# A two-layer decode block with its backward pass: the weight gradients begin inside the last attention's backward

## The chip, the core and the metric

One core of a Trainium2 chip runs the whole kernel. The metric is the device time of one execution in microseconds (us); eight executions of the kernel before have a median of 446.25 us (442.68 to 447.71). The engines are TensorE (PE; its weight loads are shown apart, as PEld), VectorE (DVE), ScalarE (ACT), GpSimd (Pool) and SyncE (SP), which here only issues DMAs. Each runs its own instructions in order and waits on semaphores for the others. SP issues DMAs on one queue, Pool on another; both feed the same 16 DMA engines.

## The reference

Four layers act on one token x of 1024 numbers, in the order A, B, A, B, with the same weights each time:

```python
x = x + A(layernorm(x))   # q = x@wq, 32 heads over 4 kv heads, softmax over the last 4096 keys, @wo
x = x + B(layernorm(x))   # h = x@w1 + b1; h*tanh(softplus(h)) @ w2
x = x + A(layernorm(x))
x = x + B(layernorm(x))
```

The output is x and, for a given gradient of it, the gradients of x, of the k and v caches (4 x 32768 x 128 each), of wq (1024 x 4096), wo (4096 x 1024), w1 (1024 x 3584), b1 and w2 (3584 x 1024), all in bf16. Outside of the last 4096 positions a cache's gradient is zero, so 28672 of 32768 rows in `out_2` and `out_3` are plain zeros that have to be written.

## The kernel before, in words

The layers are named A1, B2, A3, B4 on the way forward; the backward pass goes B4, A3, B2, A1. Weights pass through a ring of six 512 KB buffers (`ring`) or stay on the chip (`wq_b`, most of `wo_b`, K, V). The schedule is written out by hand: the program's order is each engine's order, and only waits are added.

Zero stores are single jobs of 512 KB (112 in all, `zero_jobs`). They are spread as filler for the DMA engines. `bg_zeros` (L180) puts them on Pool's queue behind a small copy that waits for a stage's value; `zeros` (L167) and `zeros2` (L171, two jobs per DMA, from `area["zero"]` inside `wo_b`) put them on SP's queue. The table `Z` says how many go where.

The last attention's backward is `attn_bwd` with `first=False`. It computes do = g @ wo^T (steps `T`, transpose a stored block, and `M`, multiply), then dP from V (`rows_mm`), ds, its transpose (`half_T`), dq from K (`qrow`, `yq`, `qacc`, `dq_bf`), dn from wq (`nrow`, `yr`, `rows_sel2`) and g0 through `ln_bwd`. Between its steps `warm` issues matmuls whose results nobody reads.

Each weight gradient is an outer product of two layers' row vectors, two rows deep. The vectors lie as columns, so they are first spread (copies on Pool into a zeroed `spread` tile), transposed on TensorE and copied out of PSUM: that is `spread_rows` (L1038), called through `tall_left`, `tall_right` and `rows_put`. Five such preparations for dW2 and dW1 are popped by `nextprep` between the last `M` steps and behind `rows_mm`.

Behind `attn_bwd` the PSUM pools are released, one pool `pair` of four 4 KB tiles is made, and the jobs run: 14 half chunks of dW2, 16 of dW1 (woven with 8 of dV behind the first 8), 16 of dWo, 16 of dWq woven with 8 of dK. A chunk is four matmuls into two `pair` tiles and two copies into a staging slot; `evac` gives each copy to VectorE or ScalarE by running totals. Every second chunk of a weight gradient issues its store on SP (1 MB, or 896 KB for dW1). Staging slots are used in turn from the list `slots`: two in `wo_b`, two in the ring, two in V, then eight in `wq_b`. dWq has a home instead, the parts of `wq_b` in their order. dK is stored in four 1 MB DMAs behind its last chunk. The preparations for the later gradients and five zero jobs are inserted between the jobs by position.

Of the kernel before, what the change touches and what calls it, by code (L numbers as in the profile page):

```python
# [14 lines left out]
P = 128  # L15
# [8 lines left out]
def kernel(  # L24
# [142 lines left out]
    def zeros(n):  # L167
        for _ in range(min(n, len(zero_jobs))):
            nc.sync.dma_start(zero_job(1), zt[:])

    def zeros2(n):  # L171

        while n > 0 and zero_jobs:
            k = 2 if zero_jobs[0][1] % 2 == 0 else 1
            nc.sync.dma_start(zero_job(k), area["zero"][:, 0:k * ZC])
            n -= k
# [92 lines left out]
        mm(acc.col(k), lhsT, vec.to_broadcast([P, R16]), start, stop)  # L269

    def acc_tile(n):
        return pacc.tile([P, n], FP32, name="acc", tag="acc")

    def sm_tile(m, n):
        return pacc.tile([m, n], FP32, name="sm", tag="sm")

    def mm(out_ap, lhsT, rhs, start, stop, **kw):
# [75 lines left out]
    def ln_bwd(dn_ps, n32, rstd, g_col, name, nxt):  # L353

        tt = work.tile([P, 2 * TD], FP32, name="tt")
        nc.vector.tensor_copy(tt[:, 0:TD], dn_ps)
        nc.vector.tensor_mul(tt[:, TD:], tt[:, 0:TD], n32[:])
        sps = sm_tile(P, 2 * TD)
        nc.tensor.matmul(sps[:], lhsT=onesD, rhs=tt[:], start=True, stop=True)
        if nxt == "A1":  # L360
            warm(5)
        if nxt == "B2":
            hook("ln")
        ab = work.tile([P, 2], FP32, name="ab")
        nc.vector.reduce_sum(ab[:], sps[:].rearrange("p (a b) -> p a b", a=2), axis=AX.X)
        t2 = work.tile([P, TD], FP32, name="t2")
        nc.vector.scalar_tensor_tensor(out=t2[:], in0=n32[:], scalar=ab[:, 1:2], in1=tt[:, 0:TD],
                                       op0=ALU.mult, op1=ALU.subtract, reverse1=True)
        gx = work.tile([P, TD], FP32, name="gx")
        nc.vector.tensor_scalar(out=gx[:], in0=t2[:], scalar1=ab[:, 0:1], scalar2=rstd[:, 0:1], op0=ALU.subtract, op1=ALU.mult)  # L370
        g_new = keep.tile([P, TD], FP32, name=f"g_{name}")
        nc.vector.tensor_add(g_new[:], g_col[:], gx[:])
        g_bf = pair_col("g" + nxt[0], nxt, TD)
        nc.vector.tensor_copy(g_bf, g_new[:])
        return g_new, g_bf
# [278 lines left out]
    def hook(nm):  # L654
        if nm in hooks:
            hooks.pop(nm)()
# [205 lines left out]
    def attn_bwd(g_col, g_bf, lname, sv, first, nxt):  # L862
# [30 lines left out]
        def M(i):  # L893
            c = late[i]
            w = held.pop(c)
            for dch in range(TD):
                mv(dacc, 2 * c + 1, w[:, 1, dch * P:(dch + 1) * P], g_bf[:, dch:dch + 1], False, dch == TD - 1)
            if i == 1:
                for j in range(4):
                    mm(dacc.cols(j, 16)[:, 0:13:4], de[:, j * P:(j + 1) * P], ident_bf[:, 0:P:32], False, True)  # L900
            if first and i in (1, 3, 5):
                fill(1, ["V", "K", "wq"], "a")
            if not first and i:
                nextprep()

        T(0)
        for c in range(8, NR):
# [8 lines left out]
        if not first:  # L916
            after_do()
            prep.extend([
                lambda: tall_left("w2", "a", 0),
                lambda: tall_left("w2", "a", 1),  # L920
                lambda: tall_right("w2", "gB"),
                lambda: rows_put(area["R1"], 0, "nB", "rep"),
                lambda: rows_put(area["R1"], 1, "dh", "pieces"),
            ])

        for i in range(2, len(late) + 1):
            if i < len(late):
# [2 lines left out]
        if first:  # L930
            pre.extend(w2_load(c) for c in range(NB - 1))
            bg_zeros(Z["A3d"], g_bf)
            fill(100, ["V"])
        else:
            after_stream()
            zeros(Z["A1d"][0])
            zeros2(Z["A1d"][1])

        do_p = work.tile([P, 2, NO], BF16, name="do_p")
        dcols = dacc.cols(0, HQ).rearrange("p (c t) -> p t c", t=2)  # L940
# [26 lines left out]
        if first:  # L967
            fill(3, ["K", "wq"], "a")
        else:
            after_v()  # L970
            nc.sync.dma_start(area["p3"], out_5[0:P, :])
            nextprep(100)
            warm(3)
        scr = kp()
        sdp = work.tile([P, 2], FP32, name="sdp")
        lps = sm_tile(P, 1)
# [7 lines left out]
        nc.vector.tensor_copy(sd[:], lps[:])  # L984
        ds = sv["p"] if first else area["ds"]
        dsT = kp().rearrange("p (j x) -> p j x", x=P)
        qrow = acc_tile(512)
        for hf in range(2):
            hs = slice(hf * 512, (hf + 1) * 512)
            nc.vector.scalar_tensor_tensor(out=ds[:, hs], in0=hv[hf][:], scalar=sd[:, 0:1], in1=sv["p"][:, hs], op0=ALU.subtract, op1=ALU.mult)  # L990
# [1 line left out]
        if first:  # L992
            fill(100, ["K"], "av")
        else:
            warm(4)
        for hf in range(2):
            half_T(ds, dsT, hf, "va"[hf])
        for j in range(TJ):
            for c in range(NC):
                mm(qrow[32 * c:32 * c + 32, :], dsT[:, j, 32 * c:32 * c + 32], kv["K"][:, :, 4 * j + c, :],  # L1000
                   j == 0, j == TJ - 1, tile_position=(0, 32 * c))
        yq = rows_copy(qrow, "v")
        if first:
            fill(2, ["wq"], "a")
        else:
            warm(3)
        qacc = sm_tile(P, HQ)
        for g in range(G):
            mm(qacc[:, 8 * g:8 * g + 8], yq[:, g * P:(g + 1) * P], fold[:, 8 * g:8 * g + 8], g == 0, True)
# [1 line left out]
        nc.scalar.activation(dq_bf, qacc[:], ACT.Copy, scale=scale)  # L1011
        if first:
            fill(100, ["wq"], "av")
        nrow = acc_tile(512)
        for h in range(HQ):
            for half in range(2):
                row_mm(nrow, 2 * half + h % 2, dq_bf[:, h:h + 1],
                       wq_b[:, 4 * half:4 * half + 4, h // 16, (h % 16) * P:(h % 16 + 1) * P], h < 2, h >= HQ - 2)
        nps = sm_tile(P, TD)
        yr = rows_copy(nrow, "v")  # L1020
        if first:
            hook("copy")
        rows_sel2(yr, Cols8(nps, True))
# [11 lines left out]
        nc.gpsimd.dma_start(out_flat.rearrange("(n p) -> n p", p=P), rt[0:n, :])  # L1035


    def spread_rows(n, put, dst, pairwise=False):  # L1038

        sp = area["spread"][pools["sturn"] % 2]  # L1040
        pools["sturn"] += 1
        for l in range(2):
            put(sp.rearrange("p j (q x) -> p j q x", q=4), l)
        ps = psum1([P, 8, P], BF16, "rw")
        for j in range(n):
            nc.tensor.transpose(ps[:, j, :], sp[:, j, :], ident_bf[:])  # L1046
        o, i = dst, ps[:, 0:n, :].rearrange("p j x -> p (j x)")
        if pairwise:
            o, i = dst.rearrange("p (c x t) -> p c t x", x=P, t=2), ps[:, 0:n, :].rearrange("p (c t) x -> p c t x", t=2)
        evac(o, i, 0.69, 1.0, None if "pair" in pools else "a")  # L1050

    def rows_put(R, side, kind, how):

# [141 lines left out]
    def after_do():  # L1195
# [1 line left out]
        area["spread"] = [s.rearrange("p (j x) -> p j x", x=P) for s in (s0, s1)]  # L1197
        area["R1"] = r1.rearrange("p (s x) -> p s x", s=2)
        pools["sturn"] = 0
        nc.gpsimd.memset(wo_flat[:, 0:2048], 0.0)  # L1200
        area["zero"], *more = cut_up(wo_flat, 8192, (4096,) * ((NR - 4) // 2))
        nc.gpsimd.memset(area["zero"], 0.0)
        slots.extend(more)
        dw_tall("w2", TF, out_8.rearrange("(c p t) d -> c p t d", p=P, t=4))
        dw_wide(lambda: area["R1"], 256, F // 2, out_6)
# [8 lines left out]
        slots.extend(cut_up(vf, 8192, (4096,) * 2))  # L1214

    prep = []
    def nextprep(n=1):
        for _ in range(min(n, len(prep))):
            prep.pop(0)()

    Z = dict(B2a=1, B2={0: 1, 4: 1, NW2 - 2: 4}, A3=14, B4=[3, 3, 2, 2, 2, 2, 5], A3c=6, A3d=28, B4w={1: 1, 4: 1, 13: 3}, W1=0, W1m=(8, 13), A1c=3, A1d=(7, 16))


    x1 = None
# [76 lines left out]
            nc.vector.tensor_copy(db_row[:, :, t], dbps[:])  # L1301
        nc.gpsimd.dma_start(out_7.rearrange("(c x) -> c x", x=2 * P), db_row.rearrange("c p t -> c (p t)"))

    g0, g0b = attn_bwd(g1, g1b, "A1", sA1, False, "X0")
    level()
    col_out(g0b, TD, out_1[0, 0, :])
    top(None)
    pacc.release()
    pt.release()
    pools["pair"] = ctx.enter_context(tc.tile_pool(name="pair", bufs=4, space=bass.MemoryType.PSUM))  # L1310

    def r3(nm):
        return area[nm].rearrange("p (g d) -> p g d", g=G)

    slots.extend(wq_b[:, t, :, :].rearrange("p h j -> p (h j)") for t in range(TD))
    stage = {}

    def take(nm):
        stage[nm] = jobs[:]
        del jobs[:]  # L1320

    take("w")
    dkv(area["p3"], r3("do3"), sA1["p"], r3("do1"), out_3, True)
    take("v")
    dw_tall("wo", HQ, out_5.rearrange("(c p t) d -> c p t d", p=P, t=4))
    take("o")
    dkv(sA3["ds"], r3("q3"), sA1["ds"], r3("q1"), out_2, False)
    take("k")
    dw_wide(lambda: area["Rq"], 512, 2048, out_4, wq_t)
    take("q")  # L1330
    late_prep = [
        lambda: row_layout(sA3["dorep"], "do3"),
        lambda: row_layout(sA1["dorep"], "do1"),
        lambda: tall_left("wo", "o", 0),
        lambda: tall_left("wo", "o", 1),
        lambda: tall_right("wo", "gA"),
        lambda: row_layout(sA3["qrep"], "q3"),
        lambda: row_layout(sA1["qrep"], "q1"),
        lambda: rows_put(area["Rq"], 0, "nA", "rep"),
        lambda: rows_put(area["Rq"], 1, "dq", "heads"),  # L1340
        db1_out,
        x4_out,
    ]

    def weave(a, b, n):
        while a or b:
            jobs.extend(a[0:n])
            jobs.extend(b[0:1])
            del a[0:n], b[0:1]

    jobs.extend(stage["w"][:NW2 + 8])
    weave(stage["w"][NW2 + 8:], stage["v"], 1)
    jobs.extend(stage["o"])
    weave(stage["q"], stage["k"], 2)
    for at, f in zip((8, 11, 24, 27, 30, 40, 43, 46, 49, 51, 53), late_prep):
        jobs.insert(at, f)
    for at, n in ((24, 2), (27, 2), (33, 1)):
        jobs.insert(at, lambda n=n: zeros2(n))
    run(1000)
    zeros2(1000)  # L1360
    assert not zero_jobs
# [30 lines left out]
```

## Time and profile before

| | |
|---|---|
| median of 8 runs | 446.25 us (442.68 to 447.71) |
| the profiled execution | 446.17 us, of which the span of the core is 444.4 |
| PE / DVE / ACT / Pool busy | 321.7 / 235.3 / 214.5 / 66.3 us |
| HBM read, written | 70.27 MB, 99.10 MB |
| mean granted TensorE clock | 0.733 of full |

The profile is of one execution. Times in it count from the span's start. A line such as L278 is the line of a helper, so groups are told apart by their tiles: `ops` is a weight gradient's PSUM tile, `rw` a row preparation's, `tps` a weight transpose, `wps` a `warm` matmul. A row "out<-in" names the tiles; what stands in brackets is the engine's idle time just before, and who ended it. The DMA share is the mean busy share of the 16 DMA engines in a stretch.

### The profile page before, as it was taken

How to read it: one execution, taken by the hardware profiler on the slowest of the kernel's cores; microseconds unless marked ns; L12 is line 12 of the kernel's file. 1: busy time of each engine (PE TensorE's matmuls, PEld its weight loads, DVE VectorE, ACT ScalarE, POOL GpSimd, SP SyncE). 2: the span in 40 equal slices, each digit the busy share in tenths (PEclk: the TensorE clock that was granted, in tenths of full speed). 3: DMA queues.
4: the chain of work that ended last, by engine and by line, in shares of the span. 5: the costliest groups of instructions: out<-in, count | busy, mean ns of one | idle time of the engine just before them, and what ended most of it. 6: DMA issues, size and time to landing. Idle time of an engine off the chain costs nothing. (4 is left out here: it accounts for less than half of the span.)

```text
span 444.4 us, 11638 instructions
## 1 busy us (share of the span) xinstructions
PE 321.7 (72%) x5020; PEld 219.1 (49%) x5020; DVE 235.3 (53%) x487; ACT 214.5 (48%) x253; POOL 66.3 (15%) x164
## 2 busy tenths in 40 slices
PE   1555855497887979988997587795967698585850
PEld 0332524497375979975876586764431132211110
DVE  3134201187251756674547373461439989897860
ACT  1122100065142867876855242523218877796860
POOL 2000000012420312252332010117010010000000
PEclk9997555566697998998998558986985555555555
DMA  8999999999999899999999999999979999999778
GB/s 317 420 421 415 407 405 372 407 371 392 397 405 344 328 348 370 386 411 412 416 408 383 416 330 380 308 411 421 424 305 374 418 413 409 402 412 396 299 307 354
DMA packets 44336, 170.13 MB, mean 383 GB/s; under 512 B 4448, under 2 KB 11644, under 8 KB 37500
## 3 DMA queue, kind: packets, MB, share of 16 engines
q1 hardware_dynamic: 31888, 124.79, 71.0%
q0 software_dynamic: 12352, 44.58, 25.6%
q8 instruction: 39, 0.64, 0.5%
q14 instruction: 13, 0.11, 0.1%
q10 hardware_dynamic: 44, 0.01, 0.0%
HBM read 70.27 MB, written 99.10 MB: 381 GB/s over the span
## 5 line engine op out<-in xcount | busy, mean ns | idle before, releaser
L278 PEld LDWEIGHTS <-ring 128*128 128x128 bf16 (+2 forms) x1828 | 59.5, 101 | 33.9 <-DMA ring<-in_B_w_dram 12.8
L195 ACT COPY ring<-tps 128x1024 bf16<-128x1024 bf16 (+1 forms) x40 | 37.6, 962 | 29.4 <-PE tps L242 29.2
L185 POOL DMA_DIRECT2D out_dram<-zt x84 | 44.4, 532 | 39.8 <-DMA out_dram<-zt 34.3
L242 PE MATMUL tps<-ident_bf,ring 128*128 128x128 bf16 x528 | 40.0, 232 | 6.3 <-DMA ring<-in_B_w_dram 5.1
L685 ACT COPY ring<-tps 128x1024 bf16<-128x1024 bf16 x28 | 28.3, 1012 | 30.9 <-PE tps L675 23.1
L698 DVE CUSTOM_DVE_ANT_0 ring<-ring,gbc 128x1024 bf16<-128x1024 bf16 x28 | 33.7, 1220 | 15.2 <-PE acc L278 14.2
L192 DVE CAST wq_b<-ops 128x1024 bf16<-128x1024 f32 (+1 forms) x36 | 39.2, 1127 | 4.5 <-DMA out_dram<-wq_b 2.8
L195 ACT CAST wq_b<-ops 128x1024 bf16<-128x1024 f32 (+1 forms) x40 | 38.3, 1015 | 5.8 <-DMA out_dram<-wq_b 2.8
L242 PEld LDWEIGHTS <-ring 128*128 128x128 bf16 x528 | 33.7, 105 | 8.2 <-DMA ring<-in_B_w_dram 5.4
L278 PE MATMUL ops<-V 2*128 2x512 bf16 (+1 forms) x160 | 32.2, 603 | 5.7 <-DVE K L192 1.5
L192 DVE COPY ring<-tps 128x1024 bf16<-128x1024 bf16 (+1 forms) x30 | 19.6, 663 | 29.3 <-PE tps L242 28.9
L278 PEld LDWEIGHTS <-V 128*128 128x128 bf16 (+2 forms) x448 | 17.0, 102 | 33.1 <-issue 31.2
L195 ACT COPY K<-tps 128x1024 bf16<-128x1024 bf16 x17 | 16.6, 1024 | 28.9 <-PE tps L242 28.9
L278 PE MATMUL ops<-wo_b 2*128 2x512 bf16 x120 | 24.7, 570 | 8.1 <-ACT wq_b L195 3.0
L675 PE MATMUL tps<-ident_bf,ring 128*128 128x128 bf16 x224 | 24.8, 280 | 0.7 <-DMA ring<-in_B_w_dram 0.7
L278 PE MATMUL acc<-a_pair,ring 128*128 128x16 bf16 x448 | 16.0, 173 | 10.7 <-DMA ring<-in_B_w_dram 9.6
L192 DVE COPY K<-tps 128x1024 bf16<-128x1024 bf16 x15 | 10.2, 688 | 24.2 <-PE tps L242 24.2
L278 PE MATMUL q<-wq_b,nA_pair 128*32 128x512 bf16 x128 | 10.1, 439 | 17.0 <-DMA wq_b<-in_A_wq_dram 17.0
L278 PEld LDWEIGHTS <-wo_b 2*128 2x128 bf16 (+1 forms) x232 | 9.0, 99 | 26.0 <-issue 23.8
L195 ACT CAST K<-ops 128x1024 bf16<-128x1024 f32 x17 | 17.1, 1012 | 7.7 <-PE ops L278 7.5
L192 DVE CAST K<-ops 128x1024 bf16<-128x1024 f32 x15 | 18.3, 1222 | 3.3 <-PE ops L278 3.2
L294 DVE COPY ring<-acc 128x512 f32<-128x512 f32 x6 | 4.1, 691 | 28.8 <-PE acc L278 28.8
(319 smaller groups left out, 564.8 us busy)
## 6 DMA issues: line engine op xcount, KB each, us to landing
out_dram<-zt POOLq DMA_DIRECT2D x84, 512.0 KB, 10.2
ring<-in_B_w_dram SPq DMA_DIRECT2D x42, 512.0 KB, 7.6
ring<-in_B_w_dram SPq DMA_DIRECT2D x32, 448.0 KB, 6.6
out_dram<-wo_b SPq DMA_DIRECT2D x13, 1024.0 KB, 8.5
out_dram<-wq_b SPq DMA_DIRECT2D x12, 1024.0 KB, 4.9
ring<-in_A_wo_dram SPq DMA_DIRECT2D x20, 512.0 KB, 7.9
wq_b<-in_A_wq_dram SPq DMA_DIRECT2D x8, 1024.0 KB, 21.2
out_dram<-wq_b SPq DMA_DIRECT2D x7, 896.0 KB, 5.2
```

The source lines that it names most:

```text
L185: nc.gpsimd.dma_start(zero_job(1), zt[:])
L192: nc.vector.tensor_copy(out_ap, in_ap)
L195: nc.scalar.copy(out_ap, in_ap)
L242: nc.tensor.transpose(ps[:, b, :], ap, ident_bf[:])
L278: nc.tensor.matmul(out_ap, lhsT=lhsT, rhs=rhs, start=start, stop=stop, skip_group_check=True, **kw)
L294: nc.vector.tensor_copy(yr, bank[:])
L675: nc.tensor.transpose(self.ps[c][:, b, :], w[:, 1, b * P:(b + 1) * P], ident_bf[:])
L685: nc.scalar.copy(self.w[c][:, 1, :], self.ps.pop(c)[:].rearrange("p b c -> p (b c)"))
L698: nc.vector.tensor_tensor_reduce(out=w[:, 0, :], in0=w[:, 0, :], in1=gbc[:], scale=1.0, scalar=0.0, op0=ALU.mult, op1=ALU.add, accum_out=s ...
```

## The change

`spread_rows` is cut in two: Pool's copies are put at once (`put_rows`), and the transposes and the copy out of PSUM come when `finish_rows` is called. Two puts stand ahead of the last `T`/`M` steps of the last attention, and the finishes stand behind `rows_mm`. The memset of the zero area moves from `after_do` to behind ds.

The code that made the pool `pair` and the job list becomes `tail`, which is called inside `attn_bwd` when ds is issued. From there on `acc_tile` and `sm_tile` take their tiles from `pair`, and eight calls of `run(1)` stand between the remaining steps and behind them, in place of `warm`. `wq_b` joins the slots behind `nrow` (hook `wq`), so behind the sixth chunk.

The zero jobs are dealt out anew: one less in B2's pass over w2, two less in B4, one more each in the W2 and W1 passes of the backward, 18 single jobs instead of 23 behind the loads of the last attention, and 11 instead of 5 between the weight gradients. The preparations get new positions in the job list.

```diff
     def acc_tile(n):
+        if "pair" in pools:
+            return psum1([P, n], FP32, "acc")
         return pacc.tile([P, n], FP32, name="acc", tag="acc")
...
@@ ln_bwd
         if nxt == "B2":
             hook("ln")
+        if nxt == "X0":
+            run(1)
...
@@ attn_bwd
-            if not first and i:
-                nextprep()
...
+            put_rows()
+            put_rows()
...
             after_stream()
-            zeros(Z["A1d"][0])
-            zeros2(Z["A1d"][1])
+            zeros(Z["A1d"])
...
             nc.sync.dma_start(area["p3"], out_5[0:P, :])
-            nextprep(100)
-            warm(3)
+            finish_rows()
+            put_rows()
+            finish_rows()
+            put_rows()
...
-        qrow = acc_tile(512)
+        qrow = acc_tile(512) if first else None
...
-            warm(4)
+            finish_rows()
+            put_rows()
+            nc.gpsimd.memset(area["zero"], 0.0)
+            hook("tail")
+            run(1)
         for hf in range(2):
             half_T(ds, dsT, hf, "va"[hf])
+        if not first:
+            finish_rows()
+            run(1)
+            qrow = acc_tile(512)
...
-            warm(3)
+            finish_rows()
+            run(1)
         qacc = sm_tile(P, HQ)
...
+        if not first:
+            run(1)
         nrow = acc_tile(512)
         for h in range(HQ):
+            if not first and h == HQ // 2:
+                run(1)
...
+        yr = rows_copy(nrow, "v")
+        if not first:
+            hook("wq")
+            run(1)
         nps = sm_tile(P, TD)
-        yr = rows_copy(nrow, "v")
...
@@ spread_rows
         for l in range(2):
             put(sp.rearrange("p j (q x) -> p j q x", q=4), l)
-        ps = psum1([P, 8, P], BF16, "rw")
...
+        def finish():
+            ps = psum1([P, 8, P], BF16, "rw")
+            for j in range(n):
+                nc.tensor.transpose(ps[:, j, :], sp[:, j, :], ident_bf[:])
...
+        ready.append(finish)
...
@@ after_do
-        nc.gpsimd.memset(wo_flat[:, 0:2048], 0.0)
+        for s in (s0, s1):
+            nc.gpsimd.memset(s, 0.0)
         area["zero"], *more = cut_up(wo_flat, 8192, (4096,) * ((NR - 4) // 2))
-        nc.gpsimd.memset(area["zero"], 0.0)
...
-    Z = dict(B2a=1, B2={0: 1, 4: 1, NW2 - 2: 4}, A3=14, B4=[3, 3, 2, 2, 2, 2, 5], A3c=6, A3d=28, B4w={1: 1, 4: 1, 13: 3}, W1=0, W1m=(8, 13), A1c=3, A1d=(7, 16))
+    Z = dict(B2a=1, B2={0: 1, 4: 1, NW2 - 2: 3}, A3=14, B4=[2, 2, 2, 2, 2, 2, 5], A3c=6, A3d=28, B4w={1: 1, 4: 1, 7: 1, 10: 1, 12: 2}, W1=0, W1m=(2, 8, 13), A1c=3, A1d=18)
...
+    def tail():
+        top(None)
+        pacc.release()
+        pt.release()
+        pools["pair"] = ctx.enter_context(tc.tile_pool(name="pair", bufs=4, space=bass.MemoryType.PSUM))
+        level()
...
+        base = stage["w"][:NW2 + 8] + weave(stage["w"][NW2 + 8:], stage["v"], 1) + stage["o"] + weave(stage["q"], stage["k"], 2)
+        side = {
+            8: [lambda: row_layout(sA3["dorep"], "do3")],
...
+            16: [lambda: zeros2(2)],
...
+            40: [lambda: zeros2(2)],
...
+    hooks.update(tail=tail, wq=lambda: slots.extend(wq_b[:, t, :, :].rearrange("p h j -> p (h j)") for t in range(TD)))
+    g0, g0b = attn_bwd(g1, g1b, "A1", sA1, False, "X0")
+    run(1)
+    col_out(g0b, TD, out_1[0, 0, :])
     run(1000)
```

More of the change, by code (lines that the diff above doesn't have):

```diff
@@ L271, in acc_tile @@
     def acc_tile(n):
+        if "pair" in pools:
+            return psum1([P, n], FP32, "acc")
         return pacc.tile([P, n], FP32, name="acc", tag="acc")
     def sm_tile(m, n):
+        if "pair" in pools:
+            return psum1([m, n], FP32, "sm")
         return pacc.tile([m, n], FP32, name="sm", tag="sm")
@@ L1035, in col_out, with finish_rows @@
         nc.gpsimd.dma_start(out_flat.rearrange("(n p) -> n p", p=P), rt[0:n, :])
+    ready = []
+    def finish_rows():
+        ready.pop(0)()
     def spread_rows(n, put, dst, pairwise=False):
@@ L1043, in spread_rows @@
             put(sp.rearrange("p j (q x) -> p j q x", q=4), l)
-        ps = psum1([P, 8, P], BF16, "rw")
[L1045 to L1050, printed above, removed]
+        def finish():
+            ps = psum1([P, 8, P], BF16, "rw")
+            for j in range(n):
+                nc.tensor.transpose(ps[:, j, :], sp[:, j, :], ident_bf[:])
+            o, i = dst, ps[:, 0:n, :].rearrange("p j x -> p (j x)")
+            if pairwise:
+                o, i = dst.rearrange("p (c x t) -> p c t x", x=P, t=2), ps[:, 0:n, :].rearrange("p (c t) x -> p c t x", t=2)
+            evac(o, i, 0.69, 1.0, None if "pair" in pools else "a")
+        ready.append(finish)
     def rows_put(R, side, kind, how):
@@ L1216, with put_rows @@
     prep = []
-    def nextprep(n=1):
-        for _ in range(min(n, len(prep))):
-            prep.pop(0)()
-    Z = dict(B2a=1, B2={0: 1, 4: 1, NW2 - 2: 4}, A3=14, B4=[3, 3, 2, 2, 2, 2, 5], A3c=6, A3d=28, B4w={1: 1, 4: 1, 13: 3}, W1=0, W1m=(8, 13), A1c=3, A1d=(7, 16))
+    def put_rows():
+        prep.pop(0)()
+    Z = dict(B2a=1, B2={0: 1, 4: 1, NW2 - 2: 3}, A3=14, B4=[2, 2, 2, 2, 2, 2, 5], A3c=6, A3d=28, B4w={1: 1, 4: 1, 7: 1, 10: 1, 12: 2}, W1=0, W1m=(2, 8, 13), A1c=3, A1d=18)
     x1 = None
@@ L1302, in db1_out @@
         nc.gpsimd.dma_start(out_7.rearrange("(c x) -> c x", x=2 * P), db_row.rearrange("c p t -> c (p t)"))
[L1304 to L1310, printed above, removed]
     def r3(nm):
         return area[nm].rearrange("p (g d) -> p g d", g=G)
-    slots.extend(wq_b[:, t, :, :].rearrange("p h j -> p (h j)") for t in range(TD))
     stage = {}
@@ L1320, in take @@
         del jobs[:]
[L1322 to L1343, printed above, removed]
@@ L1345, in weave @@
     def weave(a, b, n):
+        out = []
         while a or b:
-            jobs.extend(a[0:n])
-            jobs.extend(b[0:1])
+            out.extend(a[0:n])
+            out.extend(b[0:1])
             del a[0:n], b[0:1]
[L1351 to L1358, printed above, removed]
+        return out
@@ new lines, in tail @@
+    def tail():
[4 more added lines that the diff above has]
+        level()
+        take("w")
+        dkv(area["p3"], r3("do3"), sA1["p"], r3("do1"), out_3, True)
+        take("v")
+        dw_tall("wo", HQ, out_5.rearrange("(c p t) d -> c p t d", p=P, t=4))
+        take("o")
+        dkv(sA3["ds"], r3("q3"), sA1["ds"], r3("q1"), out_2, False)
+        take("k")
+        dw_wide(lambda: area["Rq"], 512, 2048, out_4, wq_t)
+        take("q")
+        base = stage["w"][:NW2 + 8] + weave(stage["w"][NW2 + 8:], stage["v"], 1) + stage["o"] + weave(stage["q"], stage["k"], 2)
+        side = {
+            8: [lambda: row_layout(sA3["dorep"], "do3")],
+            10: [lambda: row_layout(sA1["dorep"], "do1")],
+            16: [lambda: zeros2(2)],
+            20: [lambda: tall_left("wo", "o", 0)],
+            21: [lambda: tall_left("wo", "o", 1)],
+            22: [finish_rows, lambda: zeros2(2)],
+            23: [lambda: tall_right("wo", "gA")],
+            24: [finish_rows],
+            26: [finish_rows, lambda: zeros2(2)],
+            32: [lambda: zeros2(2)],
+            35: [lambda: row_layout(sA3["qrep"], "q3")],
+            37: [lambda: row_layout(sA1["qrep"], "q1"), lambda: rows_put(area["Rq"], 0, "nA", "rep")],
+            38: [lambda: rows_put(area["Rq"], 1, "dq", "heads")],
+            39: [finish_rows],
+            40: [lambda: zeros2(2)],
+            41: [finish_rows],
+            42: [db1_out],
+            43: [x4_out],
+        }
+        for k, f in enumerate(base):
+            jobs.extend(side.get(k, []))
+            jobs.append(f)
```

## The prediction

> **What bounds the kernel now.** I read the span in slices first, then each stage's busy table, then the timeline of the last attention and the chain that ended last. The slices show one resource that is hardly ever idle, the DMA engines:
>
> ```profile
> DMA  8999999999999899999999999999979999999778
> GB/s 317 420 421 415 407 405 372 407 371 392 397 405 344 328 348 370 386 411 412 416 408 383 416 330 380 308 411 421 424 305 374 418 413 409 402 412 396 299 307 354
> DMA packets 44336, 170.13 MB, mean 383 GB/s; under 512 B 4448, under 2 KB 11644, under 8 KB 37500
> ```
>
> The bytes are the same after the change. At the 416 GB/s that a full window shows they would take 409 us of the 444.4; so I count the time in which the DMA engines stand still. The busy table in stretches of 5 us (last three columns: granted TensorE clock, DMA share, GB/s) has two holes behind the middle:
>
> ```profile
> 325.00:330.00 5.00, 2.42 (x30) 1.56 (x22) 2.05 (x8) 0.00 (x0) 0.00 (x0) 0.96 0.98 406
> 330.00:335.00 5.00, 3.41 (x19) 0.88 (x20) 3.86 (x5) 3.70 (x5) 1.70 (x9) 0.50 0.20 81
> 335.00:340.00 5.00, 3.98 (x24) 1.03 (x23) 5.00 (x7) 4.64 (x6) 0.00 (x0) 0.50 1.00 415
> ...
> 410.00:415.00 5.00, 4.05 (x26) 0.95 (x26) 4.03 (x4) 4.29 (x6) 0.00 (x0) 0.50 0.81 328
> 415.00:420.00 5.00, 3.69 (x28) 0.93 (x21) 4.75 (x5) 4.54 (x6) 0.00 (x0) 0.50 0.62 256
> 420.00:425.00 5.00, 4.56 (x26) 0.98 (x29) 5.00 (x5) 4.54 (x5) 0.00 (x0) 0.50 0.82 338
> 425.00:430.00 5.00, 3.89 (x22) 0.68 (x14) 4.17 (x4) 3.92 (x5) 0.00 (x0) 0.50 0.61 254
> 430.00:435.00 5.00, 0.00 (x0) 0.00 (x0) 0.00 (x0) 0.85 (x1) 0.00 (x0) 0.50 1.00 416
> ```
>
> Hole A: the zero stores run dry at 329, the first dW2 store is issued at 333.8. In stretches of 1 us the missing shares add up to 4.15 us. Hole B, 408 to 430: 5 x (0.12 + 0.19 + 0.38 + 0.18 + 0.39) = 6.3 us. There VectorE and ScalarE (4 to 5 of 5 us) copy dWq and dK out of PSUM, and dK's 4 MB leave only behind the last copy: from 430.0 it takes 14.4 us to the end. Smaller holes lie earlier: 0.34 us at 136 to 138, 1.36 at 147 to 149, 0.8 at 257 to 267, 1.6 at 276 to 284.
>
> Why A is there, from the timeline (start, us, what, idle time before and its releaser):
>
> ```profile
> 299.57 1.80 POOL L1200 MEMSET wo_b<- 128x2048 bf16 x1 [3.96 <-PE sm L278]
> ...
> 301.31 3.51 POOL L1202 MEMSET wo_b<- 128x4096 bf16 x1
> 304.77 1.17 POOL L1082 COPY wo_b<-a_pair 128x16 bf16<-128x16 bf16 x8
> 304.85 9.04 SPq L175 DMA_DIRECT2D out_dram<-wo_b  x9
> ...
> 305.49 1.03 PE L1046 MATMUL rw<-ident_bf,wo_b 128*128 128x128 bf16 x8 [4.91 <-POOL wo_b L1082]
> ```
>
> TensorE, in order, stood 4.91 us in the first row transpose behind Pool's memset of the zero area, and all of the last attention with it. Why B is there, from the chain (start, us, what):
>
> ```profile
> 395.77 0.76 ACT wq_b L195
> 396.53 5.75 DMA out_dram<-wq_b
> 402.28 0.02 issue
> ```
>
> The first dWq copy writes a part of `wq_b` from which a dWo store still had to leave. After it only that store's two successors were queued, and the DMA ran empty 6 us later.
>
> **The change, part by part.**
>
> *Pool first, finish late.* Before `dps` two row sets are put and none is finished; the four finishes that stood there (8, 6, 4 and 8 transposes) move behind. From 300.4 the same steps with the durations of their rows: T 1.06, ScalarE copy 1.0, M 0.4, `warm(2)` 1.06, T 0.74, M 0.4, the DVE copy 0.69, M 0.36, `do_p` 0.5: `dps` at about 305.2 instead of 311.36, 6.1 us earlier. All late wo loads have landed, for VectorE has read the last by 301. The 3.51 us memset goes behind the fifth put on POOL; only g0's small store and the dWo rows follow it, and SP first needs the area behind its eighth dW store. On SP, 18 single zeros from `zt` take the place of 7 plus 16 (9 issues); they no longer wait for Pool (304.85), and p's load (L971, needed by dV much later) stands behind them. Before, there was no DMA hole at 297 to 305, so that wait itself gives nothing.
>
> *Zeros moved.* 23 zero units behind the A1 loads become 18: dry 5 x 0.524 MB / 0.416 = 6.3 us earlier, at 323. dW's phase gets 11 instead of 5. Early on, B2 loses 1, B4 loses 2, the W2 pass gains 1 and W1 gains 1. Where the DMA is full a unit costs 1.26 us wherever it is put, so only holes count. B2's unit is what nearly covers 136 to 138: +1.26. B4 is paced by TensorE (5.00 busy of 5); two units less lie between -1.7 (TensorE's one wait for a load there) and +2.5 (they come back in full); I take +0.8, near the middle. The spread in the W2 pass and W1 lies between -1.6 (it fills the hole at 276) and +1.26 (one more unit in front of loads that TensorE waits 7.9 us for in all); I take -0.5. Sum +1.5, ends -2.1 and +5.
>
> *Eight dW2 chunks inside the tail.* A chunk is 4 matmuls (0.6 us at half clock) and two copies, 1.22 us on DVE beside 1.01 on ACT (rows of 331 to 337); among others it takes 1.17 (24 chunks in the 28 us from 402). In front, three finishes: 8, 6, 4 transposes with 1.01, 0.82, 0.58 on ACT; the tail also carries two more. With 6.1 us taken off the old times, in queue order: ds done 311.8; third finish's copy 311.6; chunk 1 to 313.2, so `half_T`'s first copy, queued behind it on DVE, ends 313.6 (0.8 late), the fourth finish behind that; chunk 2 to 315.5, where store 1 goes. `qrow` 314 to 315.9, `yq` 316.6; on ACT the fifth finish (1.01) and chunk 3 (1.01) stand in front of `dq`: 318.8. Chunk 4 by 319.8 (store 2). First half of `nrow` 318.8 to 320.6, chunk 5, second half to 322.7, `yr` 323.4; chunk 6 sits in front of `sel` on TensorE and of `tt` on DVE (1.3): store 3 at 325. Chunk 7's DVE copy is ahead of `ab` (1.2); g0 about 328.5, chunk 8 and store 4 at 330. So g0 is about where it was, with eight chunks done.
>
> *Clock.* That sum holds at full clock. The skill's page "TensorE: Matmul & The Clock Gate", Part 1, has the clock at full after some 3.4 us of busy TensorE and halved after an idle window; by it the tail, with no such gap, stays full though ten `warm` matmuls go. The rows speak against it: from 330 on TensorE is busy 3.4 to 4.9 of 5 us with just these two-row chunk matmuls, and the granted clock is 0.50 for 100 us. By the rule the tail ends at 330; by the row, halved from `qrow` on, 1.9 + 1.05 + 3.64 + 1.05 + 0.36 = 8.0 us later, 338. I take 333: chain and chunks are mixed there.
>
> *Hole A after.* Dry at 323; stores 1 and 2 (2.5 us each) lie ready and last to 328; store 3 (325 to 327) to 330.5; store 4 (330 to 333) follows with at most some 2 us lost. I take 0.5 us of 4.15 left.
>
> *Hole B after.* Before, dWq began at 402.3, 5.75 of it a wait for a slot. `wq_b` now joins the staging list behind six chunks, so dW1 uses its parts 0 to 5 and the first two dWo chunks 6 and 7: all out long before dWq. Without the wait 396.5, less 8 chunks x 1.17 = 9.4, plus 3 for g0: dWq from 390. The DMA finishes what is ahead of it at 408 - 3.65 + 1.5 = 406, so 16 us of stores are queued then, against 6 before. To cover the hole takes 6 + 6.3 = 12.3. It closes, with almost 4 us to spare; I leave 0.3. The early reuse (7th store into the first slot, 8th and 9th into the next) waits for stores 1 to 3, out at 326 to 331, and comes at 335 to 340: free. Copies then end by 390 + 28 = 418, and 418 + 14.4 = 432 is below what the DMA gives.
>
> **Sum.** 444.4 - (4.15 - 0.5) - (6.3 - 0.3) + 1.5 = 436.2 of span. Around it lie 446.17 - 444.4 = 1.8 us; the profiled run is 0.1 us below the median of 446.25. So 438.0.
>
> **The rivals.**
> 1. *Hole B stays.* Tail at half clock, or copies slower among the chain's: dWq starts at 400 rather than 390 and the reserve falls from 16 to 6. For it: only 4 us to spare and DVE at 25.5 of 28 us; against: the slot wait is gone anyhow. 438 + 6 = 444.
> 2. *The hole only moves.* Zeros end at 323, and if stores 2 to 4 come as late as the old first one (334), hole A is kept; evacuation begins no earlier and B stays, while the early zeros cost: 446.2 + 0 to 1.5, 447. For it: four chunks need `dq` and `nrow` first; against: chunk 2 needs nothing of them.
> 3. *Slower: the tail is paid in series.* If every chunk is paid whole on the chain (0.6 + 1.22 + 0.3 = 2.1, x8 = 17), each late finish too (2 x 2.1), at half clock (8.0), the 18.2 us from ds (311.8) to g0 become 47: g0 at 359, copies end at 330's 82 us (70 chunks at 1.17) later, 441, plus 14.4: 455 of span. It decides from g0 = 348 (348 + 82 + 14.4 = 444.4). For it: all queues are in order and PSUM's four pair tiles turn between chain and chunks; against: each engine works on a neighbour's chunk while the chain waits. 457.
>
> **How the numbers follow.** Both holes close: 0.70, own range 434.5 to 441.5 (early zeros -2.1 to +5 about, half of it used). Rival 1: 0.16, rival 2: 0.06, rival 3: 0.08. The range 434 to 445.5 takes in rival 1 and leaves out rival 3, half of rival 2 and 0.05 of the best end. Under 444.0 (0.5%, about what this kernel's runs can tell): 0.70 and 0.10 of rival 1, 0.80. Above 448.5: rival 3 and a little of rival 2, 0.09. Between: 0.11.
>
> **What would show it.** `dps` near 305; no DMA stretch under 0.8 between 320 and 335, the first `out_8` store near 316; g0's store at 329 to 335; dWq's first copy near 390 without a DMA wait before it, and DMA at 1.0 from there to the end; a larger hole at 136 and at 147. Wrong if dWq starts past 395, if the tail's clock is 0.5 and g0 later than 340, or if the early holes grow by over 5 us.

## The result, and the profile after

The changed kernel has a median of 440.0 us (435.43 to 445.04, 11 runs) beside 446.11 us of the kernel before (32 runs): ratio 0.985, 95% interval 0.982 to 0.988. Two more measurements of it on other occasions gave 0.981 (0.976 to 0.987) and 0.988 (0.984 to 0.992). It is about 6 us faster; 438.0 was predicted, with 434 to 445.5 as the range. A ratio here is that of a kernel to the kernel before, taken over the fast executions alone, since a few in each set run 1 to 2% longer whatever the kernel; so it can differ from the quotient of two medians. The profiled execution took 436.83 us, its span 435.0.

The slices of the span after, DMA share in tenths, GB/s, and the bytes:

```profile
DMA  8999999999998999999999999999999999999996
GB/s 313 423 420 418 405 412 377 407 385 386 379 404 295 329 334 351 378 404 407 417 409 371 411 401 408 338 400 415 418 418 402 414 419 414 408 421 417 419 420 277
DMA packets 45056, 170.13 MB, mean 391 GB/s; under 512 B 4528, under 2 KB 11724, under 8 KB 38860
```

The bytes are the same. The 7s and the low GB/s in the last third are gone. The busy table of the two places that had holes (last three columns: granted TensorE clock, DMA share, GB/s):

```profile
325.00:330.00 5.00, 3.60 (x23) 0.99 (x23) 4.86 (x14) 3.57 (x5) 1.70 (x9) 0.50 0.98 410
330.00:335.00 5.00, 4.93 (x22) 0.92 (x20) 5.00 (x8) 4.41 (x6) 0.00 (x0) 0.50 0.94 390
...
410.00:415.00 5.00, 2.04 (x12) 0.34 (x11) 3.73 (x4) 3.11 (x4) 0.00 (x0) 0.50 1.01 419
415.00:420.00 5.00, 0.00 (x0) 0.00 (x0) 0.00 (x0) 0.00 (x0) 0.00 (x0) 0.50 1.01 421
```

Hole A is 5 x (0.02 + 0.06) = 0.4 us in this execution instead of 4.15. Hole B is gone: the copies (DVE, ACT) end at 413.8 instead of 430, and the DMA goes on at 1.0 without them until 431. Hole A is not gone from every execution. A second profile of the same kernel (438.67 us, span 436.9) has 5 x (0.23 + 0.28) = 2.55 us there:

```profile
325.00:330.00 5.00, 2.61 (x24) 1.35 (x24) 3.90 (x10) 2.16 (x3) 0.00 (x0) 0.84 0.77 320
330.00:335.00 5.00, 4.46 (x24) 1.07 (x22) 5.00 (x13) 4.39 (x5) 1.70 (x9) 0.50 0.72 292
```

The steps in between, from the timeline after (start, us, what, idle time before and its releaser):

```profile
301.19 0.23 PE L954 MATMUL dps<-ident_bf,do_p 128*32 128x128 bf16 x1
304.53 0.96 PE L1076 MATMUL rw<-ident_bf,wo_b 128*128 128x128 bf16 x14
...
307.25 3.51 POOL L1004 MEMSET wo_b<- 128x4096 bf16 x1
...
315.51 2.71 SPq L1170 DMA_DIRECT2D out_dram<-wo_b  x2
...
326.31 0.17 DVE L380 CAST gX_pair<-g_A 128x8 bf16<-128x8 f32 x1
```

The row transposes stand behind `rows_mm` and no longer wait for Pool, the 3.51 us memset has nobody behind it that matters, the first dW2 store leaves at 315.51 instead of 333.77, and g0 is ready at 326.3 instead of 329.8. The last entries of SP (the stores of dWq and of dK) are

```profile
389.13 23.87 SPq L1194 DMA_DIRECT2D out_dram<-wq_b  x8
413.80 4.39 SPq L1214 DMA_DIRECT2D out_dram<-K  x4
```

and in the kernel before `dps`, g0, the first dW2 store and these two entries were

```profile
311.36 0.23 PE L949 MATMUL dps<-ident_bf,do_p 128*32 128x128 bf16 x1
329.81 0.17 DVE L374 CAST gX_pair<-g_A 128x8 bf16<-128x8 f32 x1
333.77 2.69 SPq L1138 DMA_DIRECT2D out_dram<-wo_b  x2
404.82 24.84 SPq L1162 DMA_DIRECT2D out_dram<-wq_b  x8
430.87 3.81 SPq L1182 DMA_DIRECT2D out_dram<-K  x4
```

### The profile page after: what moved, and what is told of

Read it like the earlier page. It is cut to its first block, busy times and chain, and to the rows that moved or that the text cites. A ratio compares the mean times of both kernels' runs of the same rounds, so it can differ in the third digit from the quotient of the medians.

```text
span 435.0 us, 11654 instructions
## 1 busy us (share of the span) xinstructions
PE 318.6 (73%) x5010; PEld 217.1 (50%) x5010; DVE 235.8 (54%) x489; ACT 212.5 (49%) x251; POOL 66.2 (15%) x167
## 5 line engine op out<-in xcount | busy, mean ns | idle before, releaser
L242 PE MATMUL tps<-ident_bf,ring 128*128 128x128 bf16 x528 | 39.2, 230 | 4.8 <-DMA ring<-in_B_w_dram 3.6
L195 ACT CAST wq_b<-ops 128x1024 bf16<-128x1024 f32 (+1 forms) x36 | 34.9, 1012 | 3.1 <-PE ops L282 3.0
L242 PEld LDWEIGHTS <-ring 128*128 128x128 bf16 x528 | 32.7, 103 | 6.6 <-DMA ring<-in_B_w_dram 3.7
L192 DVE COPY ring<-tps 128x1024 bf16<-128x1024 bf16 (+1 forms) x30 | 19.7, 664 | 21.4 <-PE tps L242 21.0
L192 DVE CAST wq_b<-ops 128x1024 bf16<-128x1024 f32 (+1 forms) x28 | 30.7, 1120 | 0.7 <-PE ops L282 0.7
L681 PE MATMUL tps<-ident_bf,ring 128*128 128x128 bf16 x224 | 24.6, 278 | 0.7 <-DMA ring<-in_B_w_dram 0.7
L192 DVE CAST K<-ops 128x1024 bf16<-128x1024 f32 x16 | 19.5, 1220 | 3.8 <-PE ops L282 3.5
L282 PEld LDWEIGHTS <-wo_b 2*128 2x128 bf16 (+1 forms) x232 | 9.1, 98 | 23.2 <-issue 19.8
L242 PE MATMUL tps<-ident_bf,K 128*128 128x128 bf16 x256 | 19.7, 236 | 0.5 <-ACT K L195 0.3
L242 PEld LDWEIGHTS <-K 128*128 128x128 bf16 x256 | 16.6, 106 | 6.2 <-issue 6.0
## 6 DMA issues: line engine op xcount, KB each, us to landing
out_dram<-zt SPq DMA_DIRECT2D x18, 512.0 KB, 10.5
```

Of the source, the lines that this page charges most:

```text
L192: nc.vector.tensor_copy(out_ap, in_ap)
L195: nc.scalar.copy(out_ap, in_ap)
L242: nc.tensor.transpose(ps[:, b, :], ap, ident_bf[:])
L282: nc.tensor.matmul(out_ap, lhsT=lhsT, rhs=rhs, start=start, stop=stop, skip_group_check=True, **kw)
L681: nc.tensor.transpose(self.ps[c][:, b, :], w[:, 1, b * P:(b + 1) * P], ident_bf[:])
```

## The experiments

The theory was: two DMA holes with two causes; A is closed by getting the first stores out before the zeros end, B by the order of the staging slots. The rivals: that the eight chunks' head start closes B, that the chunks or Pool's earlier puts alone do everything, that the early zeros matter. Four kernels change one thing in the kernel after, and four build the change up from the kernel before. The kernel after was measured beside five of the runs; the old slot order, the chunks behind g0 and the two single causes were measured on another occasion without it, so those four are compared by their ratios to the kernel before. The "tail" is the stretch of the last attention from ds to g0. Sizes of holes are sums of the missing shares in stretches of 1 us, small ones left out; B of the kernel before is 6.4 us in this way.

**The old slot order in the changed kernel.**

```diff
-    hooks.update(tail=tail, wq=lambda: slots.extend(... for t in range(TD)))
+    hooks.update(tail=tail, wq=lambda: slots.__setitem__(slice(3, 3), [... for t in range(TD)]))
```

> The changed kernel, with the parts of wq_b put into the staging list where the old order had them (behind the six others), so that the last three dWo stores leave from parts 0 to 2 of wq_b again. Theory (the slot order closes hole B): the first dWq copy waits for a dWo store, dWq starts near 397 instead of 390, the DMA share falls under 0.9 behind 405, span about 440 and ratio to the kernel before about 0.995. Rival (the head start of eight chunks closes it): no wait, full DMA to the end, ratio 0.985 as the changed kernel.

Measured: 444.88 us, ratio 0.995 (0.992 to 0.999). ScalarE at the first dWq copies, then the busy table, of this kernel:

```profile
381.19 5.67 ACT L195 CAST wq_b<-ops 128x1024 bf16<-128x1024 f32 x6
403.39 1.93 ACT L195 CAST wq_b<-ops 128x1024 bf16<-128x1024 f32 x2 [16.53 <-DMA out_dram<-wq_b]
```

```profile
330.00:335.00 5.00, 4.83 (x22) 1.05 (x22) 5.00 (x9) 4.62 (x5) 1.09 (x8) 0.50 1.03 433
...
415.00:420.00 5.00, 4.69 (x28) 0.99 (x26) 4.91 (x5) 4.13 (x5) 0.00 (x0) 0.50 0.72 292
420.00:425.00 5.00, 4.01 (x22) 0.90 (x20) 4.20 (x4) 4.79 (x7) 0.00 (x0) 0.50 0.75 315
```

Hole A stays closed, and B is back with 8.1 us in sum, more than the 6.4 before. The copies ran further ahead and so stood longer (16.5 us) in front of the one slot that a dWo store still held. About two thirds of the gain hang on the order of a list.

**The chunks behind g0.**

```diff
             hook("tail")
-            run(1)
+            warm(4)
...
             finish_rows()
-            run(1)
             qrow = acc_tile(512)
...
-            run(1)
+            warm(3)
         qacc = sm_tile(P, HQ)
...
+    jobs.insert(6, lambda: hook("wq"))
     run(1)
     col_out(g0b, TD, out_1[0, 0, :])
```

(The calls ahead of and inside `nrow`, behind `yr` and in `ln_bwd` go too.)

> The changed kernel without the eight dW2 chunks in the tail: warm matmuls are back in two places, the chunks run behind g0, staging order and zeros as in the changed kernel. Theory: g0 some 6 us earlier than in the changed kernel (near 321), the first dW2 store near 324 instead of 315.5; the zeros are out by 322, so a DMA hole of 2 to 4 us returns there, hole B stays closed since slots are free; ratio about 0.991 against 0.985. Rival (the chunks matter only by their head start for the copies): hole B comes back as well, ratio near 1.0. Rival (the chunks do nothing, Pool's earlier puts do it all): ratio 0.985.

Measured: 438.88 us in 5 runs, ratio 0.984 (0.979 to 0.989): the time of the third theory. In the profile g0 comes at 320.6 instead of 326.3, the first dW2 store at 323.2, and the predicted hole is there (2.7 us at 320 to 324); but dWq's first store leaves at 391.35, 2.2 us after that of the profile after (389.13) and ahead of that of the changed kernel's second profile (391.98), and B stays closed:

```profile
325.00:330.00 5.00, 3.61 (x20) 0.83 (x18) 5.00 (x6) 4.23 (x5) 0.00 (x0) 0.50 1.00 415
...
410.00:415.00 5.00, 3.80 (x24) 0.83 (x23) 5.00 (x6) 4.24 (x6) 0.00 (x0) 0.50 1.01 419
415.00:420.00 5.00, 0.00 (x0) 0.00 (x0) 0.96 (x1) 0.83 (x1) 0.00 (x0) 0.50 1.01 419
```

The chunks lengthen the tail by nearly as much as they save behind it: from ds to g0 the engines of the chain do the chunks' work in their own queues. Counted from `dps`, which the chunks do not move, g0 comes at 25.1 and 26.5 us in the two profiles with chunks and at 19.7 without; dWq's first store comes at 87.9 and 89.3 us, and at 90.4 without. Beginning the weight gradients at ds, by itself, moves no time that can be measured here.

**Each cause alone, in the kernel before.** The slots reversed:

```diff
-    slots.extend(wq_b[:, t, :, :].rearrange("p h j -> p (h j)") for t in range(TD))
+    slots.extend(wq_b[:, t, :, :].rearrange("p h j -> p (h j)") for t in reversed(range(TD)))
```

> The kernel before with one line changed: the eight parts of wq_b enter the staging list in reverse, so that dWo leaves from parts 7 to 5 and dWq's first homes are free. Theory: the wait of 5.75 us before dWq goes, copies end near 424 instead of 430, hole B shrinks from 6.3 to about 1 us, hole A is as before; span about 439, ratio 0.987 to 0.990. Rival (B is set by the copies' own rate, or dWq then waits for PSUM or for later parts): ratio 0.997 to 1.0.

Measured: 442.73 us, ratio 0.994 (0.991 to 0.998), between the two expectations. ScalarE's wait for a DMA in front of dWq is gone from the profile; dWq's first store leaves at 401.7 instead of 404.8, a gain of 3.1 us and not 5.75, and B shrinks to 3.3 us. Hole A is there with 2.8 us. The wait was worth less than the chain had shown: there a "DMA" piece of 5.75 us lies between two copies. In ScalarE's own timeline of the kernel before the idle time is half of that,

```profile
392.79 6.74 ACT L195 CAST wq_b<-ops 128x1024 bf16<-128x1024 f32 x7
402.38 1.93 ACT L195 CAST wq_b<-ops 128x1024 bf16<-128x1024 f32 x2 [2.84 <-DMA out_dram<-wq_b]
```

since during the first 3 us of the piece the engines were still copying the dWo chunks behind the one that the chain follows.

Pool ahead:

```diff
+            nextprep(2)
         for i in range(2, len(late) + 1):
...
-            if not first and i:
-                nextprep()
...
-            nextprep(100)
+            for _ in range(2):
+                finish_rows()
+                nextprep()
             warm(3)
...
+            finish_rows()
+            nextprep()
+            nc.gpsimd.memset(area["zero"], 0.0)
             warm(4)
```

(Two more finishes behind `half_T` and `yq`, `spread_rows` cut in two as in the change, `A1d=23` single zeros.)

> The kernel before with only the row preparations cut in two: Pool's puts ahead, finishes behind rows_mm, the memset of the zero area behind ds, the 23 zeros there all from zt; no dW chunk in the tail, old slots, old early zeros. Theory: the last attention no longer stands 4.9 us behind Pool, dps and g0 are 5 to 6 us earlier (g0 near 324), the first dW2 store comes at 328 while the zeros last to 329, so hole A closes without any chunk in the tail; hole B stays (the wait for the slot stands): ratio 0.990 to 0.992. Rival (the stall is hidden, something else holds g0): g0 at 330, ratio 1.0.

Measured: 445.21 us, ratio 0.996 (0.993 to 0.999): less than expected, though hole A went as foreseen. The busy table, and ScalarE's waits (us in total, times, longest):

```profile
325.00:330.00 5.00, 2.64 (x17) 1.04 (x18) 3.25 (x8) 2.06 (x3) 1.70 (x9) 0.61 1.03 418
330.00:335.00 5.00, 3.86 (x20) 0.73 (x19) 5.00 (x6) 5.00 (x6) 0.00 (x0) 0.50 1.03 418
...
415.00:420.00 5.00, 3.69 (x26) 0.86 (x22) 5.00 (x5) 4.64 (x5) 0.00 (x0) 0.50 0.70 292
...
425.00:430.00 5.00, 3.33 (x18) 0.54 (x13) 3.61 (x4) 4.29 (x5) 0.00 (x0) 0.50 0.61 254
```

```profile
ACT wq_b L195 <- DMA out_dram<-wq_b: 5.6, 1, 5.6
```

Hole A is closed with no chunk in the tail, with all 23 zeros still in front of it. But dWq cannot start before a dWo store has left, so the copies wait 5.6 us instead of 2.8, and B has 7.9 us instead of 6.4: part of A's gain is given back in B.

**Both causes together, in the kernel before.** The two edits above in one kernel; no chunk in the tail, old early zeros.

> The kernel before with the two parts that single-part runs gave, together: row preparations cut in two with Pool ahead (as in e6), and wq_b's parts staged in reverse (as in e5); 23 zeros, old early zeros, no dW chunk in the tail. Theory (two holes, two causes, and each cause alone leaves the other hole to take the gain back): both holes close to under 2 us in sum, ratio 0.983 to 0.988, as the changed kernel. Rival (the head start of the eight chunks is needed for hole B): B stays above 3 us, ratio 0.990 to 0.993, the sum of e5 and e6.

Measured: 438.76 us, ratio 0.983 (0.978 to 0.987); again on another occasion,

> Pool's puts ahead and wq_b's parts staged in reverse, in the kernel before, once more: within 0.004 of the changed kernel, 0.979 to 0.987 of the kernel before.

438.71 us, 0.985 (0.980 to 0.991). The sum of the single gains would be 0.990. That lies outside the first interval and inside the second, and each single ratio is itself uncertain by over 0.003, so the times leave room for a plain sum. That one hole takes over the other's gain rests on the profiles: the wait that grew from 2.8 to 5.6 us, and B. The busy table of the first measurement:

```profile
330.00:335.00 5.00, 3.81 (x18) 0.88 (x18) 5.00 (x12) 3.60 (x4) 0.00 (x0) 0.50 1.01 428
...
410.00:415.00 5.00, 4.59 (x26) 0.90 (x22) 4.91 (x6) 4.29 (x5) 0.00 (x0) 0.50 0.85 352
415.00:420.00 5.00, 1.92 (x10) 0.33 (x9) 2.20 (x2) 3.08 (x4) 0.00 (x0) 0.50 0.79 324
```

Of the 10.5 us of A and B, 1.75 are left; in the profile of the second measurement, 1.8. The changed kernel on the same two occasions:

> The changed kernel once more, unaltered, on the chip of the next three, so that they can be set beside it: 0.982 to 0.988 of the kernel before.

> The changed kernel unaltered, to set beside the next two: 0.979 to 0.988 of the kernel before.

439.54 us, 0.981 (0.976 to 0.987), and 439.1 us, 0.988 (0.984 to 0.992). So the kernel before with these two edits is as fast as the whole change, as far as these runs tell.

**Pool's stall put back into the changed kernel.**

```diff
+            nc.gpsimd.memset(area["zero"], 0.0)
             put_rows()
             put_rows()
...
+            if not first and i:
+                finish_rows()
+                if i < 4:
+                    put_rows()
```

(The memset behind ds goes. The fifth finish stands behind `rows_mm`, none in the tail; chunks, slots and zeros as changed.)

> The changed kernel with Pool's stall put back: the memset of the zero area ahead of the puts and the finishes between the M steps and behind rows_mm, as in the old order; the eight chunks stay in the tail. Theory: dps near 307 instead of 301, first dW2 store near 321 when the zeros run dry, a hole of 0.5 to 2 us there, dWq without a wait, ratio 0.985 to 0.990: the chunks in the tail and Pool's earlier puts are two ways to the same end, either is enough. Rival (Pool's puts are the larger part): hole of over 3 us, ratio above 0.991.

Measured: 444.18 us, ratio 0.998 (0.995 to 1.002): the rival, and more. Timeline and busy table:

```profile
302.50 1.03 PE L1073 MATMUL rw<-ident_bf,wo_b 128*128 128x128 bf16 x8 [4.95 <-POOL wo_b L1111]
```

```profile
325.00:330.00 5.00, 4.13 (x60) 2.02 (x52) 3.39 (x6) 2.02 (x2) 0.00 (x0) 1.00 0.60 244
330.00:335.00 5.00, 2.84 (x23) 0.99 (x23) 3.58 (x13) 3.42 (x4) 0.90 (x4) 0.71 0.63 261
335.00:340.00 5.00, 3.14 (x16) 0.67 (x17) 5.00 (x8) 3.47 (x4) 0.80 (x6) 0.50 0.84 343
```

The stall is back with 4.95 us, and hole A with 5.8 (324 to 342). Five zeros fewer stand in front than in the kernel before. The first store leaves at 319.3, in time; the second at 325.1, when the DMA share has already fallen; the third only at 329.7, since with the chunks it takes 22.8 us from `rows_mm` (310.3) to g0 (333.1), where the kernel before took 17.0. So the chunks in the tail do not stand in for Pool's earlier puts. It also speaks for the stall as what counts in "Pool ahead": the single zeros from `zt`, which came with that edit, are in this kernel too, and the hole is there all the same.

**The early zeros.** `Z` for B2, B4, W2 and W1 as before, in the changed kernel:

```diff
-B2={0: 1, 4: 1, NW2 - 2: 3}, B4=[2, 2, ...], B4w={1: 1, 4: 1, 7: 1, 10: 1, 12: 2}, W1m=(2, 8, 13)
+B2={0: 1, 4: 1, NW2 - 2: 4}, B4=[3, 3, ...], B4w={1: 1, 4: 1, 13: 3}, W1m=(8, 13)
```

> The changed kernel with the old zero jobs in B2, B4, the W2 and the W1 pass (one job more in sum, taken from between the weight gradients); all else as changed. Theory of the prediction (taking three jobs out of B2 and B4 opened 1.3 + 0.8 us of holes, spreading them in W2 and W1 closed 0.5): holes at 135 to 140 and 147 to 155 smaller by about 2 us, holes at 260 to 282 larger by about 1, ratio 0.002 to 0.005 below the changed kernel's. Rival (early holes vary by that much from run to run, the deal makes no difference): ratio within 0.002 of the changed kernel's.

Measured: 439.53 us, ratio 0.984 (0.980 to 0.988), beside 439.54 us (0.981) of the changed kernel on that occasion: no difference that can be told. The profiles say the same: the changed kernel misses 2.15 us of DMA at 135 to 140 in the first profile (a share of 0.57) but 0.15 in the second (0.97), with the same deal, so that hole comes and goes by itself. The sign of it that the prediction named proves nothing.

**Two zeros later.** On top of the two edits, `A1d=21` and two jobs more between the weight gradients.

> The kernel before with Pool's puts ahead and wq_b's parts staged in reverse, and two zero jobs moved from behind the loads of the last attention to between the weight gradients. In the profile without this the first dW2 store was issued at 325.0 while the zeros lasted past 326, and 1.75 us of hole were left at 410 to 418. Theory: the two jobs (2.5 us) push the stores back and fill that hole, no new one opens at 325: 0.5 to 2 us less than without, 0.979 to 0.985 of the kernel before. Rival: the zeros were what covered 325 and the hole only moves there: no difference.

Measured: 439.42 us, ratio 0.990 (0.987 to 0.994), beside 438.71 (0.985) without. The hole at 410 to 422 went, as the theory said (no stretch of 1 us misses over 0.25 from 270 until the last stores run out at 433), and the time did not fall: neither expectation fits wholly, and 0.990 lies outside the range put down. Its profile has 1.5 and 0.9 us of holes at 138 to 152, in code that it shares with the others; whether they are what it lost is open. A gain of 1.75 us is below what these runs can tell.

## Why the prediction was right, and where it was not

- *What bounds the kernel: right.* Counting the time in which the DMA stands still gave the size. In the two profiles A went from 4.15 to 0.4 and B from 6.3 to 0, and the span by 9.4 us; 8.2 were predicted (436.2; measured 435.0).
- *The median: 2 us too low.* 438.0 against 440.0. The sum was made for one profiled execution; that of the changed kernel is 3.2 us below the median of its runs, that of the kernel before lay on it. So the 9.4 us are in part the luck of the draw: the medians differ by 6.1, and the second profile of the changed kernel has a span of 436.9.
- *Pool first: right, and undersized.* `dps` came at 301.2, not 305.2. From the last matmuls ahead of the stall (300.3 before, 297.5 after) to `dps` it takes 3.65 us instead of 11.0: the step is worth 7.4 us, not 6.1. The other 2.8 us had been gained before that point, 1.5 of them when the last attention began. The pieces that the prediction lists for this stretch add up to 6.2 us in series, where it takes 4.8 and does not say what overlaps. And some had been measured behind the stall at half clock. Here are the first `T` behind it before, the same `T` after, and the clock before (third column from the end):

```profile
306.31 1.06 PE L242 MATMUL tps<-ident_bf,ring 128*128 128x128 bf16 x8
297.65 0.61 PE L242 MATMUL tps<-ident_bf,ring 128*128 128x128 bf16 x8
302.00:309.00 7.00, 3.51 (x34) 2.97 (x35) 0.00 (x0) 2.44 (x3) 5.00 (x15) 0.52 1.02 415
```

- *Hole A: right in the profile, for a reason that was only half of it.* The text closes it by stores 1 and 2 out of the tail, and these came on time (store 1 predicted at 315.5, measured 315.51; store 3 at 325, measured 322.5). It did not ask whether Pool's step closes A by itself. With 23 zeros in front it does, as the run with Pool ahead alone shows; and the one with the stall put back shows that the chunks do not do it in its place. The chunks' early stores are needed only since the change also takes five zeros away from there: with 18 zeros and no chunk a hole of 2.7 us was left. The four profiles with Pool ahead, 21 or 23 zeros and no chunk have no hole A of over 0.4 us; with 18 zeros and chunks two of four have one of over 2 us (the second profile of the changed kernel and that with the old early zeros).
- *The chunks in the tail: the terms were nearly right, and what they say was missed.* "Less 8 chunks x 1.17 = 9.4, plus 3 for g0" reads like a head start of 6.4 us. But g0 is put 3 us later than before although Pool's step takes 6.1 off, so the chunks are charged with 9.1 us and keep 0.3; the rest of the 6.4 is Pool's. The profiles give a cost of 5.4 and 6.8 us in the tail and a net of 2.5 and 1.1 (25.1 and 26.5 against 19.7 us to g0; 87.9 and 89.3 against 90.4 to dWq's first store). So the part that gives the change its name was worth next to nothing by the prediction's own sum, clock term included, and kernels without it are as fast.
- *Hole B: right in cause, wrong in the term.* "5.75 of it a wait for a slot" was read from the chain; the engine waits 2.84, and removing the wait alone is worth 3.1. dWq's first copy came at 385.6, not 390, since the tail started earlier; counted from `dps` it is 84.4 us, and 84.8 had been put. That agreement is in part luck: the wait was put too long, and the chunks' net too low. That the wait grows when all else gets faster (5.6 and 16.5 us) the text did not see; it makes the slot order a condition for all the rest.
- *The early zeros: not shown.* +1.5 us was the estimate. The larger hole at 135 that it named as a sign is in one profile of the changed kernel and not in the other, and the kernel with the old deal is no faster.
- *The clock: about the size taken, and not the same twice.* From `dps` to g0, in the profile after, in the second profile of the same kernel, with the old slot order (which changes nothing in the tail), and without the chunks (the third column from the end is the granted clock):

```profile
301.20:326.30 25.10, 20.19 (x242) 10.06 (x242) 15.64 (x27) 12.05 (x15) 5.55 (x15) 0.86 1.03 417
302.70:329.20 26.50, 21.12 (x242) 10.04 (x242) 15.68 (x28) 12.04 (x15) 5.55 (x15) 0.86 1.00 409
304.50:327.70 23.20, 17.82 (x242) 9.34 (x242) 15.65 (x28) 12.05 (x15) 5.55 (x15) 0.99 1.03 418
300.90:320.60 19.70, 15.90 (x221) 9.16 (x221) 7.44 (x20) 5.09 (x8) 5.55 (x15) 1.00 1.02 414
```

  At full clock the chunks cost 3.5 us (23.2 against 19.7), and stretches at half clock another 1.9 and 3.3. The prediction added 3 for the clock, between the page's rule and its own row, and did not foresee that it varies. By that rule alone (the Trainium skill, "TensorE: Matmul & The Clock Gate", Part 1: half clock after an idle window of about 3.4 us) the tail would have stayed at full clock, for TensorE waits no longer than 1.43 us at a time there; one of these three profiles with chunks agrees, two do not. In the profile after the clock is 0.50 at 309 to 312 and from 322.8 on, in the second at 312 to 314, 318.6 to 321.3 and from 328.7 on; there the third dW2 store goes at 325.8, not 322.5, and hole A is open. What sets these stretches was not tried. The row that spoke against the rule was misread in one point: from 330 to 430 the kernel before has TensorE busy for 1.8 to 4.9 of 5 us, not 3.4 to 4.9; the clock is 0.50 throughout, as the text says.
- *The rivals.* "Hole B stays" did not happen. The changed kernel with the old slot order ends where that rival would have (444.9, put at 444), but for the slot, which the rival took as settled, and not for a late tail. "The hole only moves" has the right mechanism, stores 2 to 4 too late for the zeros: the run with the stall put back is such a case (444.2, put at 447), and the second profile of the changed kernel is a mild one. The series of chunk and chain, the slower case, is far off: 18.9 us from ds to g0 against 47.

## What to carry to other kernels

Where one resource is busy nearly all the time, list each stretch in which it stands still, and find each one's own cause: closing one hole can let the next one take the gain back. Here two edits of 2.6 and 1.9 us, each poor alone, were worth 6.5 to 7.8 together (each figure is uncertain by 1.5 us or more). Before work is woven into a chain to fill a hole, look at what the chain itself is queued behind; here a memset in front of the copies that mattered made hole A. And subtract what the chain pays for the woven work from what is saved behind it. A piece of a chain that ends in a DMA is not an engine's idle time: read the wait from that engine's row.

## What was not expected of the hardware

Kernels with the very same code and zeros up to there reach the gradient behind B4 at 189.5 us (the kernel before) and at 192.6, 193.0, 188.7, 191.1 and 192.1 (the five profiles of kernels that were built up from it): 4.3 us between six executions, as much as the smaller effects here, and none of it from the edits, which come later. What sets it was not tried.

The granted clock of the same code differs from one execution to the next as well: with chunks in the tail it was 0.86, 0.86 and 0.99 from `dps` to g0 in the three profiles above, and the same 32 matmuls of `nrow`'s first half took 1.91 us in one and 3.59 in another. In the kernels built up from the kernel before, with `warm` matmuls there and no chunk, it was 0.98 to 1.00.
